# Attention with its strided units first, and expert 0 in three groups of 384 tokens

## The chip, the cores and the metric

One core of one Trainium2 chip runs the whole program. The metric is the device time of one execution in microseconds (us). The engines are called as in the profile: PE is the matrix engine (PEld its weight loads), DVE the vector engine, ACT the scalar engine, POOL the general one, and SP the engine whose queue issues most of the transfers (DMAs).

## The reference

Three layers follow each other. Attention has 2 batches, 8 heads, 576 positions of width 64; heads 0 to 3 see the last 32 positions ("local"), heads 4 to 7 see the earlier positions of the same class modulo 32 ("strided"). The 1152 rows of width 512 that come out of it go through a dense mixture of 8 experts, weighted by a matrix P that 8 rounds of row and column scaling make. Its result goes through a second mixture that picks two experts for each token.

```python
scores = scale * np.matmul(q, k.transpose(0, 1, 3, 2))            # per head, masked local or strided
attn = softmax(np.where(masks, scores, -1e9))
x = np.matmul(attn, v)                                            # -> [1152, 512]
logits = x @ w_gate
P = np.exp(logits - logits.max())
for _ in range(8):
    P /= P.sum(1, keepdims=True) + 1e-09
    P /= P.sum(0, keepdims=True) + 1e-09
    P *= N / E
for e in range(E):
    out += P[:, e:e + 1] * (np.maximum(x @ w1[e], 0.0) @ w2[e])   # 8 experts, all tokens
...                                                               # then the layer with the two best experts
```

## The kernel before

**Precision.** Each product of the experts is three matmuls: `split` (L99) makes a high and a low part of an operand (ACT writes the high part at L101 or L104, DVE the low part at L102 or L106), and `mm3` (L162) multiplies high with high, low with high and high with low.

**Attention** is cut into units. A `local_unit` (L262) is one batch, one pair of heads and three blocks of 64 queries; a `strided_unit` (L282) is one batch, both strided pairs of heads and four (the last time three) blocks of 54. A unit goes through: scores on PE into a bank of PSUM (`scores`, L223), the maximum on DVE (L241), an exponential on ACT for each block (L247), the scaling on DVE (L251), a transpose on PE (L271 or L290), a copy by ACT or DVE (L258, L260), the product with the values on PE (L277, L298), and `split` into `xh` and `xl`, whose four chunks are the two local and the two strided pairs. A batch has six local units (three of pair 0, then three of pair 1) and then three strided ones; `attention(0)` stands ahead of `attention(1)` (L316). Ahead of the first scores PE does 16 filler matmuls (`hum`, L219).

**Loads.** `load_pair` (L186) issues q, k and the values of a pair as transfers of their own on SP's queue, which goes in order: a transfer whose place is not free yet holds up those behind it. The first pair of batch 0 comes in two cuts. The local queries, and the strided ones of batch 1, lie in the part of `acc` (from its fifth tile of 128 tokens on) that is not used yet.

**Expert 0** of the dense layer runs beside attention. Its inner width 1024 is cut into four quarters `q`: `fetch_u` loads 1 MB of weights, `conv_u1` and `conv_u2` split them, `pair1` (L621) makes hidden values for a group of tokens, `pair2` (L630) adds their product to `acc`, tile by tile. First come all four quarters for the `early` tokens 0 to 511 (tiles 0 to 3), behind `attention(1)` in the program; then the gate (`gate_logits`, `sinkhorn`: eight rounds that make P); then the four quarters again for the `late` tokens in two groups of 320 (tiles 4 to 8). The conversions of quarter 0 stand on ACT behind the ninth `split` (`firsts[8]`), a split of the second strided unit of batch 0, and those of quarter 1 and later behind the twelfth.

**Sums.** Experts 1 to 6 use products of quarter blocks, for which `sums` (L667) makes four sums of the blocks of x in two steps `c`: eight additions on DVE into `r`, then four `split`s of it. Both steps' splits stand on ACT behind the second late quarter (`marks[1]`), and their work on DVE behind the first `split` of the hidden values (`lows[0]`).

**Order.** Up to the last expert of the dense layer, the order of each engine's instructions is made when the program is built, by priority (program order, with the gate and `sinkhorn` raised) and modelled times; what is emitted in the end runs in order on each engine. `issue_after` adds an edge on one engine only: an instruction that stands in its block waits for one that is named, if both are on the same engine.

Of the kernel before, what the change touches and what calls it, by code (L numbers as in the profile page):

```python
# [59 lines left out]


@with_exitstack
def tile_kernel(ctx: ExitStack, tc: tile.TileContext, qL, kL, vL, qS, kS, vS, wg, u12, w1, w2, wgn, noise, v1, v2, cst, masks, dummy, out):
    nc = tc.nc
    cpool = ctx.enter_context(tc.tile_pool(name="cpool", bufs=1))
    dram = ctx.enter_context(tc.tile_pool(name="dram", bufs=1, space=bass.MemoryType.DRAM))
# [111 lines left out]
    fold2 = cpool.tile([128, 2 * E], F32, name="fold2")  # L178
    fold = apool.tile([64, E], F32, name="fold", bufs=1)
    flip = [0, 0]  # L180
    where = [0, "ad", None]
    spread = [apool.tile([128, 4, 2, 64], F32, name=f"spread{i}", bufs=1) for i in range(2)]
    for x in spread:
        nc.gpsimd.memset(x, 0.0)

    def load_pair(b, hp):  # L186
        local = hp < 2
        nq, nk, nb, q, k, v = (NQ, LK, NJ, qL, kL, vL) if local else (GK, GK, NG, qS, kS, vS)
        hp %= 2
        flip[1] = (flip[1] + 1) % 4  # L190
        qs = acc[:, 4:].rearrange("p t d -> p (t d)")[:, flip[1] * 640:flip[1] * 640 + nb * nq]
        w = k.shape[-1]
        if b == 0 and not local:
            qs = pre.tile([128, NG * GK], F32, name=f"qs{hp}")
            ks = pre.tile([128, S + STRIDE], F32, name=f"ks{hp}")
        else:
            ks = apool.tile([128, S + STRIDE], F32, tag="ks", name="ks")
        if local or hp == 0:
            where[2] = (pre if b == 0 and not local else apool).tile([128, NG, 128], F32, tag="vs", name="vs")
        vs, n = where[2], v.shape[-2]  # L200
        if b == 0 and hp == 0 and local:
            cut = 3 * nq
            nc.sync.dma_start(ks[:, :224], k[b, hp, :, :224])
            nc.sync.dma_start(qs[:, :cut], q[b, hp, :, :cut])
            nc.sync.dma_start(ks[:, 224:w], k[b, hp, :, 224:])
            nc.sync.dma_start(qs[:, cut:], q[b, hp, :, cut:])
        else:
            nc.sync.dma_start(ks[:, :w], k[b, hp])
            nc.sync.dma_start(qs, q[b, hp])

        def values():
            if local:
                nc.sync.dma_start(vs[:, :n], v[b, hp])
            elif hp == 1:
                nc.sync.dma_start(vs[:, :n], v[b])

        return (qs, ks, vs), values

    def hum(o, n):  # L219
        for _ in range(n):  # L220
# [38 lines left out]
        else:  # L259
            nc.vector.tensor_copy(o, i)  # L260

    def local_unit(b, hp, j0, nb, got):  # L262
        qs, ks, vs = got
        first = maskb[:, M_ML:M_MS].rearrange("p (b k) -> p b k", b=3)
        mask = first if j0 == 0 else first[:, 1:2].to_broadcast([128, nb, LK])
        scv = scores(NQ, LK, mask, j0, nb, qs, ks, NQ)
        s = apool.tile([128, 1, 3, LK], F32, tag="s", name="s", bufs=3)
        weights_of([scv], s)
        tr = ps("b", "tr")
        for i in range(nb):  # L270
            nc.tensor.transpose(tr[:LK, i * 128:(i + 1) * 128], s[:, 0, i], ident)  # L271
        at = apool.tile([128, 4 * 2 * GK], F32, tag="at", name="at", bufs=3)
        take(at, tr, LK, NQ, nb)
        ot = ps("c", "ot")
        for i in range(nb):
# [6 lines left out]
    def strided_unit(b, j0, nb, pairs):  # L282
        mask = maskb[:, None, M_MS:].to_broadcast([128, nb, GK])
        scv = [scores(GK, GK, mask, j0, nb, qs, ks, GK) for qs, ks, _ in pairs]
        vs = pairs[0][2]
# [19 lines left out]
    def load_first():  # L305
        pairs, queue = [], []
        for hp in range(4):
            got, values = load_pair(0, hp)
            pairs.append(got)
            if queue:  # L310
                queue.pop(0)()
            queue.append(values)
        queue.pop()()
        return pairs

    def attention(b):  # L316
        pairs = load_first() if b == 0 else []

        def get(hp):
            while hp >= len(pairs):  # L320
                got, values = load_pair(b, len(pairs))
                values()
                pairs.append(got)
            return pairs[hp]

        for hp in range(2):
            for j0, nb in LOCAL:
                local_unit(b, hp, j0, nb, get(hp))
        get(3)
        for j0, nb in STRIDED:  # L330
            strided_unit(b, j0, nb, pairs[2:])

    mask_sb = apool.tile([128, NMASK // 2], F32, name="mask_sb", bufs=1)
    nc.scalar.dma_start(mask_sb, masks)
# [15 lines left out]
    nc.gpsimd.tensor_tensor(fold2, ident[:, :2 * E], ident[:, 32:32 + 2 * E], op=ALU.add)  # L350
    for j in (64, 96):
        nc.gpsimd.tensor_tensor(fold2, fold2, ident[:, j:j + 2 * E], op=ALU.add)
    where[1] = "a"
    attention(1)
    split(wg2[:, :, :E], wg2[:, :, 32:32 + E], wg_sb)

# [258 lines left out]
        return xg  # L615

    whole = ((0, 384), (384, 384), (768, 384))
    early = ((0, 512),)
    late = ((512, 320), (832, 320))

    def pair1(w, groups):  # L621
        wh, wl = w
# [23 lines left out]

    for q in range(NP):
        raw = fetch_u(0, q)
        with tc.issue_after(firsts[min(q, 1) * 3 + 8].ins):
            a, b = conv_u1(raw[0]), conv_u2(raw[1])  # L650
        pair1(a, early)
        for t in range(4):
            pair2(b, t, None, q == 0)
    tags[:] = ["a", "c"]
    with tc.high_priority(1500):
# [11 lines left out]
    def sums():  # L667
        with tc.tile_pool(name="tpool", bufs=1, side="right", reuse_waits="tile") as tpool:
            for c in range(2):
                r = tpool.tile([128, 4, HALF], F32, tag="r", name="r")  # L670
                for i in range(4):
                    nc.vector.tensor_tensor(r[:, i], quarter[0][i][:, c].bitcast(F32), quarter[1][i][:, c].bitcast(F32), op=ALU.add)
                for o, x, y, op in ((3, 2, 3, ALU.add), (2, 0, 2, ALU.subtract), (0, 3, 0, ALU.subtract), (1, 1, 0, ALU.subtract)):
                    nc.vector.tensor_tensor(r[:, o], r[:, x], r[:, y], op=op)
                for k, i in enumerate((3, 0, 2, 1)):
                    split(sh[:, k, c], sl[:, k, c], r[:, i])

    marks = []
    for q in range(NP):
        q = NP - 1 - q  # L680
        if q < NP - 1:
            raw = fetch_u(0, q)
            a, b = conv_u1(raw[0]), conv_u2(raw[1])
        pair1(a, late)
        for t in range(4, NT):
            pair2(b, t, None, q == NP - 1)
        marks.append(seen[0].ins)
    with tc.issue_after(marks[1]), tc.issue_after(lows[0].ins):
        sums()
    with tc.issue_after(seen[0].ins):  # L690
        nc.scalar.dma_start(wgn_sb, wgn)
        nc.scalar.dma_start(noise_sb, noise)
# [438 lines left out]
                down(ws[2:], [tt], [OVER], 0)  # L1131


_HOST = ["qL", "kL", "vL", "qS", "kS", "vS", "wg", "u12", "w1", "w2", "wgn", "noise", "v1", "v2", "cst", "masks", "dummy"]


def layout(x):
# [10 lines left out]
    def keys(a):  # L1148
        return a.transpose(0, 1, 3, 2).reshape(B, 2, 2 * D, a.shape[2])
# [25 lines left out]
    for j in range(3):  # L1175
# [15 lines left out]
    d = dict(qL=keys(q[:, :4]), kL=keys(kL), vL=values(vL, LK, NQ),  # L1191
             qS=keys(qS), kS=keys(kS), vS=values(vS, GK, GK).reshape(B, 128, NG, 2 * D), wg=rows(x["moe_w_gate"]),
             u12=np.stack([x["moe_w1"].reshape(E, NC, 128, NP, 256).transpose(0, 3, 2, 1, 4).reshape(E, NP, 128, 2, 512),
                           x["moe_w2"].reshape(E, NP, 2, 128, DM).transpose(0, 1, 3, 2, 4)], 3).reshape(E, NP, 128, 4, 512),
             w1=w1t(x["moe_w1"])[E - 1:], w2=w2t(x["moe_w2"])[E - 1:],
# [19 lines left out]
```

## Time and profile before

| | us |
|---|---|
| median of 3 runs (lowest to highest) | 1104.33 (1103.67 to 1104.60) |
| the profiled execution, its own time | 1105.53 |
| its span in the trace | 1103.7 |
| PE busy in the span | 1085.4 |
| DVE busy | 661.6 |
| ACT busy | 396.5 |

The trace covers the span; 1.8 us of the profiled execution's time lie around it. "Busy" is the union of an engine's instructions; of a matmul the end is modelled. The granted clock is 1.00 at 2.4 GHz and falls to 0.5 at 1.2 GHz, so that a mean of 0.9 over a stretch says that a fifth of it was at the lower level. Stages of interest: attention until about 83 us, the early part of expert 0 from 33.8 to 103.7 us, the late part until about 163 us, and experts 1 to 6 after it.

### The profile page before, as it was taken

The numbers are of one execution on the slowest core, as the hardware profiler recorded it, in microseconds if no ns is written. First come the engines' busy times: TensorE is split into PE (matmuls) and PEld (weight loads), VectorE is DVE, ScalarE is ACT, GpSimd is POOL, SyncE is SP. The second block draws the span as 40 slices with busy tenths as digits, with TensorE's granted clock in tenths as the row PEclk, the third lists the DMA queues.
The fourth block names the chain that finished last, engine by engine and source line by source line (L and its number), as shares of the span: only waits on it lengthen the run. The fifth ranks groups of instructions, "written<-read, shape, count | busy, mean of one in ns | idle before, by whom it ended". The sixth has DMA issues, their size and how long they took to land.

```text
span 1103.7 us, 17178 instructions
## 1 busy us (share of the span) xinstructions
PE 1085.4 (98%) x6840; PEld 954.5 (86%) x6840; DVE 661.6 (60%) x1359; ACT 396.5 (36%) x893; POOL 158.8 (14%) x182
## 2 busy tenths in 40 slices
PE   9999999999999999999999999999999999999996
PEld 6778988999899999899999999988888888888885
DVE  6865896666666666666666666554266465445440
ACT  6641334332322333322332332222133254444541
POOL 1000112111111111121111120000041432232211
PEclk9999999999999999999999999999999999999998
DMA  9321162111111121111121111122103674666531
GB/s 349 133 77 39 39 198 67 39 71 44 40 39 39 39 78 39 39 39 39 39 77 39 39 39 39 39 77 77 39 21 125 181 256 106 205 204 205 185 99 24
DMA packets 31589, 98.18 MB, mean 89 GB/s; under 512 B 6482, under 2 KB 15186, under 8 KB 22928
## 3 DMA queue, kind: packets, MB, share of 16 engines
q1 hardware_dynamic: 16192, 78.94, 19.7%
q0 software_dynamic: 5408, 11.26, 4.9%
q10 hardware_dynamic: 9904, 6.83, 2.0%
q8 instruction: 55, 0.90, 0.3%
q14 instruction: 30, 0.25, 0.1%
HBM read 85.51 MB, written 11.60 MB: 88 GB/s over the span
## 4 chain that ended last, share of the span: by engine, by line
PE 90%; DVE 3%; DMA 2%; ACT 2%; issue 1%; POOL 1%; POOLq 0%; SPq 0%; ACTq 0%
PE y L164 42%; PE h L164 17%; PE a L715 14%; PE b L715 7%; PE d L715 3%; PE y L892 2%; PE xgt L800 1%; PE sc L232 1%; ACT spread L247 1%; DMA raw<-in_v 1%; DMA xg<-x2d,tt 1%; DVE wl L106 1%; PE sc L221 0%; POOL table L548 0%; PE lgT L367 0%
## 5 line engine op out<-in xcount | busy, mean ns | idle before, releaser
L641 DVE SCALAR_TENSOR_TENSOR acc<-y,P,acc 128x512 f32<-128x512 f32 x207 | 152.8, 748 | 142.8 <-PE y L164 142.7
L164 PE MATMUL y<-u2h,gh 128*128 128x512 f32 x504 | 199.0, 395 | 0.6 <-DVE acc L641 0.3
L164 PE MATMUL y<-u2l,gh 128*128 128x512 f32 x504 | 197.8, 392 | 0.0
L164 PE MATMUL y<-u2h,gl 128*128 128x512 f32 x504 | 190.6, 393 | 0.8 <-DVE gl L102 0.8
L154 POOL TENSOR_TENSOR ut<-raw 128x256 f32<-128x256 f32 x48 | 36.5, 782 | 554.0 <-DVE u1l L106 446.0
L164 PEld LDWEIGHTS y<-u2h,gl 128*128 128x128 f32 x504 | 94.8, 189 | 20.8 <-DVE gl L102 1.6
L164 PE MATMUL h<-xh,wh 128*128 128x384 f32 (+8 forms) x352 | 110.2, 313 | 0.2 <-DVE hl L102 0.2
L164 PE MATMUL h<-xl,wh 128*128 128x384 f32 (+8 forms) x352 | 110.2, 313 | 0.0
L164 PE MATMUL h<-xh,wl 128*128 128x384 f32 (+8 forms) x352 | 109.8, 312 | 0.0
L164 PEld LDWEIGHTS y<-u2h,gh 128*128 128x128 f32 x504 | 95.1, 189 | 16.2 <-issue 0.7
L164 PEld LDWEIGHTS y<-u2l,gh 128*128 128x128 f32 x504 | 95.0, 188 | 14.1
L101 ACT ACTIVATE hh<-h 128x256 fp32r<-128x256 f32 (+2 forms) x88 | 35.6, 415 | 95.5 <-PE h L164 95.5
L164 PEld LDWEIGHTS h<-xh,wh 128*128 128x128 f32 x352 | 66.4, 189 | 1.1 <-DVE hl L102 0.5
L164 PEld LDWEIGHTS h<-xl,wh 128*128 128x128 f32 x352 | 66.4, 189 | 0.9 <-issue 0.4
L104 ACT ACTIVATE u2h<-raw 128x1024 fp32r<-128x1024 f32 x31 | 33.0, 1064 | 94.5 <-PE y L164 90.8
L164 PEld LDWEIGHTS h<-xh,wl 128*128 128x128 f32 x352 | 66.4, 189 | 0.0
L102 DVE SCALAR_TENSOR_TENSOR hl<-h,hh 128x256 fp32r<-128x256 f32 (+2 forms) x88 | 40.3, 465 | 41.2 <-ACT hh L101 41.2
L106 DVE TENSOR_TENSOR wl<-raw,wh 128x1024 fp32r<-128x1024 f32 x42 | 49.5, 1221 | 22.8 <-ACT wh L104 22.8
L715 PE MATMUL b<-sh,u1h 128*128 128x288 f32 x192 | 57.5, 299 | 0.0
L715 PE MATMUL b<-sl,u1h 128*128 128x288 f32 x192 | 57.5, 299 | 0.0
L715 PE MATMUL b<-sh,u1l 128*128 128x288 f32 x192 | 57.4, 299 | 0.0
L715 PE MATMUL a<-sh,u1l 128*128 128x288 f32 x192 | 57.0, 297 | 0.0
(257 smaller groups left out, 2453.9 us busy)
## 6 DMA issues: line engine op xcount, KB each, us to landing
raw<-in_u SPq DMA_DIRECT2D x31, 1024.0 KB, 4.8
raw<-in_v SPq DMA_DIRECT2D x20, 1024.0 KB, 8.9
acc<-in_v SPq DMA_DIRECT2D x12, 1024.0 KB, 6.8
raw<-in_w SPq DMA_DIRECT2D x4, 1024.0 KB, 4.9
out<-zero ACTq DMA_DIRECT2D x1, 3072.0 KB, 18.2
vs<-in_vL SPq DMA_DIRECT2D x4, 576.0 KB, 7.1
x2d<-acc ACTq DMA_DIRECT2D x9, 256.0 KB, 2.0
vs<-in_vS SPq DMA_DIRECT2D x2, 704.0 KB, 6.5
```

Source lines behind the costliest of these rows:

```text
L101: seen[0] = nc.scalar.activation(hi, src, AF.Relu)
L102: lows.append(nc.vector.scalar_tensor_tensor(lo, src, 0.0, hi.bitcast(F32), op0=ALU.max, op1=ALU.subtract))
L104: seen[0] = nc.scalar.activation(hi, src, AF.Copy)
L106: nc.vector.tensor_tensor(lo, src, hi.bitcast(F32), op=ALU.subtract)
L154: nc.gpsimd.tensor_tensor(t[:, o], x, y, op=ALU.subtract)
L164: nc.tensor.matmul(o, a, b, start=start, stop=stop)
L232: nc.tensor.matmul(sc[h * 64:h * 64 + w, i * nk:(i + 1) * nk], qs[r, j * w:(j + 1) * w], ks[r, j * step:j * step + nk], start=False, stop= ...
L247: nc.scalar.activation(s[:, x, i], v[:, i], AF.Exp, scale=0.125, bias=nmx[:, k:k + 1], accum_out=sm[:, k:k + 1])
L641: nc.vector.scalar_tensor_tensor(acc[:, t], p, P[:, t, scale:scale + 1], acc[:, t], op0=ALU.mult, op1=ALU.add)
L715: nc.tensor.matmul(p, l[:, b, c], m, start=first and i == 0, stop=i == 5, skip_group_check=not first)
L800: nc.tensor.transpose(p[:, o:o + 128], xg[:, c * 128:(c + 1) * 128], ident)
L892: nc.tensor.matmul(p[j * w:j * w + k, :d], hr[:, f, :k], raws[f // 4][:, f % 4, j * d:(j + 1) * d], start=f == 0, stop=f == 7)
```

## The change

- `attention(b)` does the three strided units first, then the local units by block group: both pairs of heads for blocks 0 to 2, then for blocks 3 to 5, then for 6 to 8.
- q and k of a pair come in one transfer into one tile (`xS`, `xL`, laid out on the host): the strided ones in tiles of their own, in batch 0 cut so that the columns of the first unit come first; the local ones in the free part of `acc`. There are three tiles for values.
- The scores take PSUM banks of one tag only (`where[1] = "a"`) from the second local group of batch 0 on (before: from batch 1 on).
- Expert 0's tokens are grouped as 384 early (tiles 0 to 2) and two times 384 late (tiles 3 to 8).
- The conversions of quarter 0 stand behind the fifth and the seventh `split`, later quarters' behind the eleventh.
- `sums` is ordered in two steps: the splits of step c on ACT behind `marks[c]`; the edge to `lows[0]` on DVE is gone.

```diff
-    def load_pair(b, hp):
...
+    def load(x, src, cut=0):
+        if cut:
+            nc.sync.dma_start(x[:, :, :cut], src[:, :, :cut])
+            return partial(nc.sync.dma_start, x[:, :, cut:], src[:, :, cut:])
+        nc.sync.dma_start(x, src)
+
+    def load_strided(b):
+        xs, rest = [], []
+        for hp in range(2):
+            if b == 0:
+                x = pre.tile([128, 2, NG * GK], F32, name=f"x{hp}")
+            else:
+                x = apool.tile([128, 2, NG * GK], F32, tag="x", name="x")
+            rest.append(load(x, xS[b, hp], (1 - b) * STRIDED[0][1] * GK))
+            xs.append(x)
+        for f in rest:
+            if f:
+                f()
+        vs = (pre if b == 0 else apool).tile([128, NG, 128], F32, tag="vs", name="vs", bufs=1 if b == 0 else 3)
+        return xs, vs, partial(nc.sync.dma_start, vs, vS[b])
+
+    def load_local(b):
+        xs, vs = [], []
+        for hp in range(2):
+            x = acc[:, 4:].rearrange("p t d -> p (t d)")[:, hp * 1280:hp * 1280 + 2 * S + STRIDE]
+            load(x, xL[b, hp])
+            xs.append((x[:, :S], x[:, S:]))
+        for hp in range(2):
+            v = apool.tile([128, NG, 128], F32, tag="vs", name="vs", bufs=3)
+            load(v[:, :NJ], vL[b, hp])
+            vs.append(v)
+        return xs, vs
...
     def attention(b):
-        pairs = load_first() if b == 0 else []
...
-        for hp in range(2):
-            for j0, nb in LOCAL:
-                local_unit(b, hp, j0, nb, get(hp))
-        get(3)
+        xs, vs, values = load_strided(b)
+        values()
+        lx, lv = load_local(b)
         for j0, nb in STRIDED:
-            strided_unit(b, j0, nb, pairs[2:])
+            strided_unit(b, j0, nb, xs, vs)
+        for j0, nb in LOCAL:
+            if j0:
+                where[1] = "a"
+            for hp in range(2):
+                local_unit(b, hp, j0, nb, *lx[hp], lv[hp])
...
-    where[1] = "a"
     attention(1)
...
     whole = ((0, 384), (384, 384), (768, 384))
-    early = ((0, 512),)
-    late = ((512, 320), (832, 320))
+    early = whole[:1]
+    late = whole[1:]
...
-        with tc.issue_after(firsts[min(q, 1) * 3 + 8].ins):
-            a, b = conv_u1(raw[0]), conv_u2(raw[1])
+        with tc.issue_after(firsts[10 if q else 4].ins):
+            a = conv_u1(raw[0])
+        with tc.issue_after(firsts[10 if q else 6].ins):
+            b = conv_u2(raw[1])
         pair1(a, early)
-        for t in range(4):
+        for t in range(3):
             pair2(b, t, None, q == 0)
...
             for c in range(2):
-                r = tpool.tile([128, 4, HALF], F32, tag="r", name="r")
...
+                with tc.issue_after(marks[c]):
+                    r = tpool.tile([128, 4, HALF], F32, tag="r", name="r")
...
         pair1(a, late)
-        for t in range(4, NT):
+        for t in range(3, NT):
             pair2(b, t, None, q == NP - 1)
         marks.append(seen[0].ins)
-    with tc.issue_after(marks[1]), tc.issue_after(lows[0].ins):
-        sums()
+    sums()
```

## Rows read from the trace of the kernel before

**Rows 1.** Busy us of PE, PEld, DVE, ACT, POOL by stretch; then clock, DMA.
```profile
6.20:20.00 13.80, 13.30 (x235) 10.04 (x234) 10.11 (x42) 10.47 (x59) 0.00 (x0) 1.00 1.04 412
20.00:33.80 13.80, 12.19 (x206) 9.03 (x203) 12.04 (x41) 12.41 (x61) 1.04 (x5) 0.92 0.66 246
33.80:61.00 27.20, 27.20 (x245) 20.93 (x244) 21.30 (x52) 14.53 (x55) 0.00 (x0) 0.98 0.44 155
61.00:73.00 12.00, 10.76 (x120) 7.96 (x118) 8.08 (x19) 7.61 (x36) 0.00 (x0) 0.86 0.01 1
73.00:103.70 30.70, 30.70 (x170) 23.71 (x168) 18.32 (x33) 6.26 (x10) 0.00 (x0) 1.00 0.20 70
103.70:128.00 24.30, 24.30 (x145) 22.57 (x145) 15.71 (x49) 5.74 (x12) 0.05 (x1) 1.00 0.13 44
128.00:142.00 14.00, 13.98 (x78) 12.33 (x77) 13.54 (x24) 5.94 (x11) 3.78 (x4) 1.00 0.03 5
142.00:158.00 16.00, 15.42 (x88) 13.60 (x87) 15.76 (x35) 6.89 (x12) 4.44 (x4) 1.00 0.61 195
158.00:180.00 22.00, 20.10 (x113) 17.71 (x112) 16.77 (x47) 7.58 (x16) 3.90 (x4) 0.92 0.61 188
```

**Rows 2.** Waits of PE until 240 us: total us, times, longest.
```profile
PE cs L395 <- DVE c L393: 1.5, 1, 1.5
PE sc L227 <- ACT spread L247: 1.1, 2, 0.6
```

**Rows 3.** Chain of waits, pieces in order of time: start us, us, what.
```profile
86.15 2.76 PE y L164 x12
...
91.22 5.60 PE h L164 x24
...
108.38 1.76 PE h L164 x12
```

**Rows 4.** The tile ot: all 24 low parts, first and last start.
```profile
L106 DVE TENSOR_TENSOR xl<-ot,xh x24: 305/389/564, 14.8 to 83.4; 128x192 fp32r<-128x192 f32 x12, 128x216 fp32r<-128x216 f32 x8, 128x144 fp32r<-128x144 f32 x4
```

**Rows 5.** Timeline of PE and of ACT: first matmul of expert 0, first exponential.
```profile
33.83 0.78 PE L164 MATMUL h<-xh,u1h 128*128 128x512 f32 x1
...
8.18 0.34 ACT L247 ACTIVATE s<-sc,nmx 128x96 f32<-128x96 f32 x1 [6.16 <-DVE nmx L242]
```

**Rows 6.** Group of the local exponentials, 6 to 34 us: busy us, mean ns.
```profile
L247 ACT ACTIVATE s<-sc,nmx 128x96 f32<-128x96 f32 x27 | 8.8, 353 | 6.4 <-DVE nmx L242 6.2 <-DVE sm L248 0.3
```

**Rows 7.** Groups of DVE, 33.8 to 103.7 us: busy us, mean ns, idle before.
```profile
L645 DVE TENSOR_TENSOR acc<-y,acc 128x512 f32<-128x512 f32 x12 | 8.2, 686 | 5.1 <-PE y L164 5.1
L106 DVE TENSOR_TENSOR u2l<-raw,u2h 128x1024 fp32r<-128x1024 f32 x5 | 6.1, 1220 | 0.4 <-ACT u2h L104 0.4
L106 DVE TENSOR_TENSOR u1l<-raw,u1h 128x512 fp32r<-128x512 f32 x9 | 6.0, 684 | 2.7 <-ACT u1h L104 2.7
L102 DVE SCALAR_TENSOR_TENSOR gl<-h,gh 128x512 fp32r<-128x512 f32 x8 | 5.5, 686 | 6.5 <-ACT gh L101 6.5
```

**Rows 8.** The tile r of the sums: times of one, first and last start.
```profile
L672 DVE TENSOR_TENSOR r<-xh,xl x8: 741/745/753, 42.0 to 138.7; 128x576 f32<-128x576 f32 x8
...
L104 ACT ACTIVATE sh<-r x8: 667/672/691, 129.2 to 147.3; 128x576 fp32r<-128x576 f32 x8
L106 DVE TENSOR_TENSOR sl<-r,sh x8: 741/746/1292, 131.4 to 151.8; 128x576 fp32r<-128x576 f32 x8
```

**Rows 9.** The matmul of each round of sinkhorn, two instructions a round.
```profile
L395 PE MATMUL cs<-c,onesr x16: 170/256/278, 110.2 to 171.1; 128*128 128x8 f32 x16
```

**Rows 10.** SP's queue in order of time, and its DMA issues by size.
```profile
1.65 0.42 SPq L205 DMA_DIRECT2D ks<-in_kL  x1
...
12.12 1.07 SPq L133 DMA_DIRECT2D raw<-in_u  x2
13.66 0.33 SPq L208 DMA_DIRECT2D ks<-in_kL  x1
...
ks<-in_kL SPq DMA_DIRECT2D x1, 192.0 KB, 3.8
```

More of the change, by code (lines that the diff above doesn't have):

```diff
@@ L62, in tile_kernel @@
 @with_exitstack
-def tile_kernel(ctx: ExitStack, tc: tile.TileContext, qL, kL, vL, qS, kS, vS, wg, u12, w1, w2, wgn, noise, v1, v2, cst, masks, dummy, out):
+def tile_kernel(ctx: ExitStack, tc: tile.TileContext, xL, vL, xS, vS, wg, u12, w1, w2, wgn, noise, v1, v2, cst, masks, dummy, out):
     nc = tc.nc
@@ L180, in tile_kernel @@
     flip = [0, 0]
-    where = [0, "ad", None]
+    where = [0, "ad"]
     spread = [apool.tile([128, 4, 2, 64], F32, name=f"spread{i}", bufs=1) for i in range(2)]
@@ L184, in tile_kernel @@
         nc.gpsimd.memset(x, 0.0)
-    def load_pair(b, hp):
[L187 to L217, printed above, removed]
@@ L260, in take, with local_unit @@
             nc.vector.tensor_copy(o, i)
-    def local_unit(b, hp, j0, nb, got):
-        qs, ks, vs = got
+    def local_unit(b, hp, j0, nb, qs, ks, vs):
         first = maskb[:, M_ML:M_MS].rearrange("p (b k) -> p b k", b=3)
@@ L280, in local_unit, with strided_unit @@
         split(xh[:, hp, o], xl[:, hp, o], ot[:, :nb * NQ])
-    def strided_unit(b, j0, nb, pairs):
+    def strided_unit(b, j0, nb, xs, vs):
         mask = maskb[:, None, M_MS:].to_broadcast([128, nb, GK])
-        scv = [scores(GK, GK, mask, j0, nb, qs, ks, GK) for qs, ks, _ in pairs]
-        vs = pairs[0][2]
+        scv = [scores(GK, GK, mask, j0, nb, x[:, 0], x[:, 1], GK) for x in xs]
         wide = spread[where[0] // 2 % 2]
@@ L303, in strided_unit @@
             split(view[0][:, r0:r1], view[1][:, r0:r1], ot[:, :(r1 - r0) * NI].rearrange("p (r i) -> p r i", i=NI))
[L305 to L314, printed above, removed]
-    def attention(b):
-        pairs = load_first() if b == 0 else []
[L319 to L324, printed above, removed]
-        for hp in range(2):
-            for j0, nb in LOCAL:
-                local_unit(b, hp, j0, nb, get(hp))
-        get(3)
-        for j0, nb in STRIDED:
-            strided_unit(b, j0, nb, pairs[2:])
+    def attention(b):
+        xs, vs, values = load_strided(b)
+        values()
+        lx, lv = load_local(b)
+        for j0, nb in STRIDED:
+            strided_unit(b, j0, nb, xs, vs)
[4 more added lines that the diff above has]
+                local_unit(b, hp, j0, nb, *lx[hp], lv[hp])
     mask_sb = apool.tile([128, NMASK // 2], F32, name="mask_sb", bufs=1)
@@ L669, in sums @@
             for c in range(2):
-                r = tpool.tile([128, 4, HALF], F32, tag="r", name="r")
[L671 to L676, printed above, removed]
+                with tc.issue_after(marks[c]):
+                    r = tpool.tile([128, 4, HALF], F32, tag="r", name="r")
+                    for i in range(4):
+                        nc.vector.tensor_tensor(r[:, i], quarter[0][i][:, c].bitcast(F32), quarter[1][i][:, c].bitcast(F32), op=ALU.add)
+                    for o, x, y, op in ((3, 2, 3, ALU.add), (2, 0, 2, ALU.subtract), (0, 3, 0, ALU.subtract), (1, 1, 0, ALU.subtract)):
+                        nc.vector.tensor_tensor(r[:, o], r[:, x], r[:, y], op=op)
+                    for k, i in enumerate((3, 0, 2, 1)):
+                        split(sh[:, k, c], sl[:, k, c], r[:, i])
     marks = []
@@ L1131, in tile_kernel @@
                 down(ws[2:], [tt], [OVER], 0)
-_HOST = ["qL", "kL", "vL", "qS", "kS", "vS", "wg", "u12", "w1", "w2", "wgn", "noise", "v1", "v2", "cst", "masks", "dummy"]
+_HOST = ["xL", "vL", "xS", "vS", "wg", "u12", "w1", "w2", "wgn", "noise", "v1", "v2", "cst", "masks", "dummy"]
 def layout(x):
@@ L1190, in layout @@
     dummy[:, 0] = np.arange(E * ROWS) % ROWS % PAD
-    d = dict(qL=keys(q[:, :4]), kL=keys(kL), vL=values(vL, LK, NQ),
-             qS=keys(qS), kS=keys(kS), vS=values(vS, GK, GK).reshape(B, 128, NG, 2 * D), wg=rows(x["moe_w_gate"]),
+    d = dict(xL=np.concatenate([keys(q[:, :4]), keys(kL)], 3), vL=values(vL, LK, NQ),
+             xS=np.stack([keys(qS), keys(kS)], 3), vS=values(vS, GK, GK).reshape(B, 128, NG, 2 * D), wg=rows(x["moe_w_gate"]),
              u12=np.stack([x["moe_w1"].reshape(E, NC, 128, NP, 256).transpose(0, 3, 2, 1, 4).reshape(E, NP, 128, 2, 512),
```

## The prediction

> **What bounds the kernel now.** I read the stretches first, then what ends PE's waits, then single tiles. Over the span PE is busy 1085.4 of 1103.7 us, and the change touches only the first 180 us or so, so the question is how much of PE's time there is idle or at the lower clock. [rows 1] gives it. From 6.2 to 33.8 us PE is idle 0.50 + 1.61 = 2.1 us, and the granted clock 0.92 in the second stretch stands for 0.16 x 13.8 = 2.2 us at the lower level, so 1.1 us of work lost: 3.2 us together. From 33.8 to 61 us nothing is idle (0.5 us lost to the clock). From 61 to 73 us it is 1.24 idle and (1 - 0.86) x 12 = 1.7 to the clock, 2.9 together. From 73 to 142 us, nothing to speak of. From 142 to 180 us it is 0.58 + 1.90 idle and 0.08 x 22 = 1.8 to the clock: 4.2 together. The lower level, 1.2 in place of 2.4 GHz, comes each time in a stretch in which PE also pauses. All that a better order of the same work can win is 3.2 + 0.5 + 2.9 + 4.2 = 10.8 us.
>
> Who holds PE up differs by stage. Until 33.8 us, when expert 0's first matmul starts [rows 5], ACT and DVE carry the attention (ACT 12.41, DVE 12.04 of 13.8 us [rows 1]). At 61 to 73 us PE waits for the banks of strided scores, which ACT's exponentials free [rows 2]. From 128 to 158 us DVE is full (13.54 of 14 and 15.76 of 16 us), after only 15.71 of 24.3 us in the stretch ahead of it [rows 1]; the longest wait is for sinkhorn's column sum on DVE, 1.5 us [rows 2].
>
> **PE's own work: no change.** A matmul of 512 columns takes 5.60/24 = 0.2333 us and one of 320 takes 1.76/12 = 0.1467 us [rows 3]; on the line through both, 384 columns take 0.1754 us. A hidden value is 12 matmuls a group, 8 times: before 96 x (0.2333 + 2 x 0.1467) = 50.6 us, after 96 x 3 x 0.1754 = 50.5. The tiles of `pair2` stay nine a quarter at 2.76/2 = 1.38 us each [rows 3]. What moves is the balance: early work was 96 x 0.2333 + 16 x 1.38 = 44.5 us and becomes 96 x 0.1754 + 12 x 1.38 = 33.4 us; late work grows by the same 11.1.
>
> **The start: about 0.5 us won.** Expert 0 now needs seven of batch 0's nine units, not all. ACT is busy 22.9 us between its first exponential at 8.2 us and 33.8 us [rows 1, 5], idle 2.7. Of this 9 of the 27 local exponentials (8.8 x 9/27 = 2.9 us [rows 6]) are of batch 1, and about 2.4 us quarter 0's conversions (taken as DVE's halves of them, 2 x 0.68 + 1.22 [rows 7], a little less). The two units that may come later are 6 exponentials (2.0 us) and about 1 us of copies. So the first matmul can come at 8.2 + (22.9 - 2.9 - 2.4 - 3.0) + 2.4 + 2.7 = 27.9 us, 5.9 us earlier. This is not 5.9 us won: PE was busy 25.5 of those 27.6 us with attention, some of it batch 1's, and what isn't done by 28 us is done later. Only the 3.2 us of waste can go. The strided units come first with 8 exponentials ahead of the first transpose, which gives PE less to do early; so I take 0.5, between -2 (the first 14 us, with 0.5 us idle now, get as thin as the next 14) and +3.2.
>
> **The loads: nothing.** The first unit now needs two transfers of 128 x 432 x 4 B = 216 KB in place of some 208 KB. The third transfer of before (400 KB in all by then) was issued at 1.65 us and landed 3.8 us later, at 5.45 us [rows 10]; 432 KB land by about 5.6, and the fillers keep PE until 6.2 us. The cover is 0.6 us thin; without it each 0.1 us costs 0.1. Later transfers follow at 412 GB/s [rows 1]: the rest of q and k and the strided values by 10 us, all 4.3 MB of batch 0 by about 15, ahead of the local units, which ACT reaches after 22 strided exponentials. Batch 1's strided tiles no longer share a place with local ones, so those two waits of SP go.
>
> **The middle: 1.5 us won.** After 28 us PE has 33.4 us of early work and about 20 us of attention left: PE's busy time from 6.2 to 103.7 us less the losses, the early work and the gate's matmuls leaves some 40 us for both batches, and 18 to 20 of it are done by 28 us. So it lasts until about 82 us. DVE's share of that: one batch and two units, about 17.5 + 3, and of the experts 12 additions (0.6 each to the next), 8 low parts (about 0.47) and three quarters' conversions [rows 7], 18: together 38.5 of 54 us, 71%, as 47.7 of 69.9 us, 68%, now [rows 1]. The burst of strided exponentials that held PE up at 61 us still comes, three times, but at about 30 to 45 us, while two quarters of hidden values lie ready as filler. I take half of 2.9, between -3 (DVE is late with hidden values) and +2.9.
>
> **The sums: 3.8 us won.** r is there from 42 us on, but its first split on ACT starts only at 129.2 us, behind the second late quarter, and the second step follows until 152 us [rows 8]: 8 low parts, 4 second-step additions and 4 combinations, 16 x 0.7 = 11 us of DVE in a stretch where it is full, with sinkhorn's rounds between them (16 matmuls from 110.2 to 171.1 us, 7.6 us a round [rows 9]). After the change the first step's splits come behind the first late quarter, one quarter or 8.4 + 8.3 = 16.7 us of PE time earlier than behind the second, and the second step's additions with them. The gate comes earlier too, since batch 1 ends earlier, so sinkhorn should be done before the sums of expert 1 are wanted, and the wait of 1.5 us with the slow clock behind it goes. Late work is 11.1 us longer on PE, so DVE has more time in all. I take 3.8 of 4.2, between 0 and 4.2. The dropped edge to `lows[0]` costs at most two additions of 0.7 us early on; DVE has room.
>
> **Sum.** 0.5 + 1.5 + 3.8 = 5.8 us. Against the profiled execution's own 1105.5 (1103.7 of span and 1.8 around it) that is 1099.7; the median of the runs is 1.2 us below that execution, so 1098.5. The bounds of the parts give +5 and -10.3; the forecast's own range is 1095 to 1102.
>
> **A rule that says more.** PEld is busy 10.04 of 13.8 and 9.03 of 13.8 us in the attention, 73% and 65%, but 22.57 of 24.3, 93%, where only experts run [rows 1]. If the small matmuls leave such room, PE's 97% before 20 us is no bound, and the 5.9 us of the earlier start count in full: 5.9 + 1.5 + 3.8 = 11.2, 1093. The Trainium skill, "Perfetto Trace Analysis", section "Identifying the Most-Contended Engine", says that the busy share of matmuls is a poor measure of headroom and that the busy share of weight loads should be read instead.
>
> **Rivals.**
> - *More, 1093* (12%): as just worked out. Against it: the waits of PE before 33.8 us are only 2 us.
> - *Given back, 1104* (18%): DVE's load is only moved, and what the sums leave at 150 us comes back at 28 to 60 us, where all of batch 1 (20.5 us with the two units) and two quarters of expert work (9 us) want DVE in 32 us, 92%. Then 3.8 + 0.5 is met by 3 to 4 of new waits for low parts. For it: PE's wait for DVE's low parts is the pattern of 142 to 158 us. Against it: from 33.8 to 61 us DVE was at 78% without an idle PE.
> - *Slower, 1107.7* (15%): batch 1's local q and k go into places that batch 0's last local scores read, and these now come last, at about 25 us. If the planner puts those transfers ahead of quarter 0's or 1's weights on SP, the queue stands until then, 2.4 MB take 5.9 us, the weights 2.5 us a quarter and 2 to land, the conversions 2.4: the first matmul comes at 38 us, not 28. PE has some 4 of the 10 us filled by batch 1's strided units and loses about 1.2 to the clock: 6 + 1.2 - 3.8 = 3.4 us slower, 1107.7. It decides from the point where the weights are issued behind about 20 us. Against it: before, the weights (12.12 us) went ahead of transfers that stand earlier in the program (13.66) [rows 10]. The same sign has the case that early work ends before batch 1 does: its last low part came at 83.4 us [rows 4], 49.6 us after expert 0's start, and with the same lag comes at 77.5, 4.5 us ahead of 82.
>
> **Numbers.** Forecast 55%. Faster by over 0.2% (2.2 us, about what a measurement of this kernel can tell from none) is 0.53 of the forecast's 0.55, the 0.12 and a little of "given back": 0.67. Same: most of "given back", 0.17. Slower: 0.16. A range that leaves out some 10% at each end is 1092 to 1107.5.
>
> **What would show it.** Right: expert 0's first matmul at 26 to 30 us; the first `sh` split near 95 us in place of 129.2; sinkhorn's last matmul before 150 us; PE idle under 0.5 us in the last late quarter and at expert 1's start. Wrong: raw weights landing after 25 us; PE waiting for `gl` or for `spread` at 30 to 60 us; a pause of PE between the early and the late part; a mean clock below 0.9 in any of these.

## The result and the profile after

| | before | after |
|---|---|---|
| median of 5 runs (lowest to highest), us | 1104.33 (1103.67 to 1105.72) | 1114.23 (1109.55 to 1115.20) |
| ratio, with its 95% interval | | 1.0081 (1.0061 to 1.0100) |
| the profiled execution, own time / span, us | 1105.53 / 1103.7 | 1115.20 / 1113.4 |
| mean granted clock over the span | 0.992 | 0.984 |

The change makes the kernel 0.8% slower, some 9.9 us by the medians; 1098.5 was forecast. Most of it is lost before 200 us. The same stretches as in [rows 1], and one more:

```profile
6.20:20.00 13.80, 11.99 (x185) 8.56 (x183) 7.62 (x29) 9.03 (x57) 0.00 (x0) 0.88 1.03 419
20.00:33.80 13.80, 11.29 (x160) 8.26 (x160) 10.03 (x33) 8.89 (x37) 0.00 (x0) 0.76 0.54 205
33.80:61.00 27.20, 26.77 (x273) 21.14 (x270) 18.48 (x49) 17.58 (x77) 2.26 (x5) 0.74 0.36 128
61.00:73.00 12.00, 12.00 (x140) 9.50 (x139) 10.43 (x31) 7.30 (x27) 0.00 (x0) 1.00 0.24 89
73.00:103.70 30.70, 30.28 (x197) 24.45 (x196) 21.24 (x45) 8.65 (x24) 0.00 (x0) 1.00 0.19 69
...
128.00:142.00 14.00, 14.00 (x72) 12.65 (x72) 12.64 (x25) 5.50 (x10) 3.33 (x4) 1.00 0.69 216
142.00:158.00 16.00, 16.00 (x83) 14.63 (x82) 12.63 (x31) 4.56 (x8) 2.94 (x4) 1.00 0.67 201
158.00:180.00 22.00, 20.28 (x115) 18.07 (x114) 16.94 (x48) 5.95 (x11) 2.87 (x4) 1.00 0.26 96
180.00:200.00 20.00, 20.00 (x110) 17.96 (x109) 11.22 (x22) 10.16 (x21) 2.87 (x4) 0.91 0.01 1
```

Read PE's busy time (the first number behind the length) and the clock (the third from the end) against [rows 1]. From 6.2 to 61 us PE is idle 1.81 + 2.51 + 0.43 = 4.8 us, where it was 2.1 before, and the clock takes (0.12 + 0.24) x 13.8 + 0.26 x 27.2 = 12.0 us, where it took 1.6. That is 13.1 us more lost. From 61 to 73 us nothing is lost any more: 2.9 us won, more than forecast. At 128 to 158 us DVE is no longer full and PE never idle. But the wait behind it has only moved: 1.72 us idle at 158 to 180, again for sinkhorn's column sum (`cs`, last line of the waits below), and 0.09 x 20 = 1.8 us of clock behind that, 3.5 in place of 4.2. Together with 0.4 us idle at 73 to 104 us the sum is 13.1 - 2.9 - 0.7 + 0.4 = 9.9 us. Counted from one event to the same event it is less: the 100th matmul of expert 1's products starts at 197.2 us instead of 188.8, which is 8.4 us, and the last 1.3 of the span's 9.7 us arise later. What lies between the 9.9 and the 8.4 us is not explained.

The clock's largest piece is one unbroken stretch at the lower of its two levels:

```profile
30.70:47.80 17.10, 16.67 (x145) 12.82 (x146) 11.58 (x29) 9.90 (x38) 2.26 (x5) 0.50 0.47 166
```

PE is busy 16.67 of its 17.10 us, so in a view of busy time this stretch looks full; it takes the granted clock to see that the work runs at half speed. PE's timeline shows the pauses for banks of scores that came before it, and what ended it (start, duration, instruction, and in brackets the pause ahead of it):

```profile
10.98 0.23 PE L227 MATMUL sc<-mask_sb 128*128 128x162 bf16 x1 [0.59 <-ACT spread L247]
...
12.13 0.23 PE L227 MATMUL sc<-mask_sb 128*128 128x162 bf16 x1 [0.48 <-ACT spread L247]
...
13.27 0.28 PE L227 MATMUL sc<-mask_sb 128*128 128x288 bf16 x1 [0.48 <-ACT spread L247]
...
21.44 0.28 PE L227 MATMUL sc<-mask_sb 128*128 128x288 bf16 x1 [0.57 <-ACT s L247]
...
28.97 0.25 PE L227 MATMUL sc<-mask_sb 128*128 128x216 bf16 x1 [0.56 <-ACT s L247]
...
30.43 0.25 PE L227 MATMUL sc<-mask_sb 128*128 128x216 bf16 x1 [0.67 <-ACT s L247]
...
36.64 1.01 PE L164 MATMUL h<-xh,u1h 128*128 128x384 f32 x2 [0.43 <-ACT xh L104]
37.58 1.55 PE L276 MATMUL ot<-at,vs 96*64 96x64 f32 x24
...
46.71 0.52 PE L164 MATMUL h<-xh,u1l 128*128 128x384 f32 x1
47.03 0.52 PE L164 MATMUL h<-xh,u1h 128*128 128x384 f32 x1
...
48.43 0.34 PE L164 MATMUL h<-xl,u1h 128*128 128x384 f32 x1
48.61 0.34 PE L164 MATMUL h<-xh,u1l 128*128 128x384 f32 x1
```

Two pauses of 0.56 and 0.67 us for banks of scores come right ahead of it. Through it PE runs the attention's matmuls of 54 to 96 columns, its transposes and masks, and a few of expert 0's between them. Most of expert 0's are recorded with 0.52 us each here, and with 0.34 us at full clock. The clock is back at 47.8 us, after expert 0's matmuls of 384 columns have run in one piece since 46.23 us. The first of them, which was to start at 27.9 us, starts at 36.64 (before: 33.83 [rows 5]).

PE's longest waits until 50 us (total, times, longest) are for what ACT's exponentials free, strided (`spread`) and local (`s`); the last line is the wait for sinkhorn between 150 and 200 us:

```profile
PE sc L227 <- ACT s L247: 1.8, 3, 0.7
PE sc L227 <- ACT spread L247: 1.6, 3, 0.6
...
PE cs L376 <- DVE c L374: 1.7, 1, 1.7
```

The sums did move. The splits of r start at 115.9 us in place of 129.2, and the last low part starts at 139.2 in place of 151.8 us [rows 8]; yet sinkhorn's last matmul, at 171.1 us before [rows 9], is at 179.3 now:

```profile
L104 ACT ACTIVATE sh<-r x8: 669/672/675, 115.9 to 135.9; 128x576 fp32r<-128x576 f32 x8
L106 DVE TENSOR_TENSOR sl<-r,sh x8: 742/746/747, 118.1 to 139.2; 128x576 fp32r<-128x576 f32 x8
...
L376 PE MATMUL cs<-c,onesr x16: 170/256/277, 108.9 to 179.3; 128*128 128x8 f32 x16
```

### The profile page after: what moved, and what is told of

Same layout as the page of the kernel before. It is cut to its first block, busy times and chain, and to the rows that moved or that the text cites. A ratio compares the mean times of both kernels' runs of the same rounds, so it can differ in the third digit from the quotient of the medians.

```text
span 1113.4 us, 17155 instructions
## 1 busy us (share of the span) xinstructions
PE 1092.7 (98%) x6840; PEld 963.5 (87%) x6840; DVE 662.9 (60%) x1359; ACT 396.6 (36%) x893; POOL 156.6 (14%) x182
## 4 chain that ended last, share of the span: by engine, by line
PE 91%; DVE 3%; DMA 2%; ACT 1%; issue 1%; POOL 1%; POOLq 0%; SPq 0%; ACTq 0%
PE y L164 42%; PE h L164 17%; PE a L698 14%; PE b L698 7%; PE d L698 3%; PE y L875 2%; PE sc L232 1%; PE xgt L783 1%; DMA xg<-x2d,tt 1%; DMA raw<-in_v 1%; PE ot L276 1%; DVE wl L106 1%; PE sc L221 1%; POOL table L529 1%; ACT spread L247 0%
## 5 line engine op out<-in xcount | busy, mean ns | idle before, releaser
L698 PE MATMUL a<-sh,u1h 128*128 128x288 f32 x192 | 57.1, 297 | 0.0
```

The costliest lines, as they stand in the source:

```text
L698: nc.tensor.matmul(p, l[:, b, c], m, start=first and i == 0, stop=i == 5, skip_group_check=not first)
```

## The experiments

Ratios are to the kernel before on the same chip, with 95% intervals. The kernel before itself had medians of 1105.24, 1104.68 and 1106.97 us beside the three groups of runs, so medians of different groups are not compared directly, only the ratios.

### Which part of the change costs it

**The sums in two steps alone**, on the kernel before:

```diff
             for c in range(2):
+                with tc.issue_after(marks[c]):
...
-    with tc.issue_after(marks[1]), tc.issue_after(lows[0].ins):
-        sums()
+    sums()
```

> The kernel before with one part of the change alone: the sums in two steps (each step's splits behind its own late quarter, no edge on DVE). If the forecast of the sums holds, DVE's full stretch after 128 us thins out and the 4.2 us that PE loses at 142 to 180 us shrink to about 0.4: 1100.5, ratio 0.9965. If sinkhorn's last rounds stay just ahead of expert 1's sums whatever the sums do, the wait for its column sum and the slow clock behind it stay, and the time is 1103 to 1104.5 (ratio 0.999 to 1.000). If the two steps themselves cost time, it is over 1106.

Measured: 1103.92 us, 0.9994 (0.9984 to 1.0003). No difference that the interval allows to call one.

**The groups of 384 alone**, on the kernel before:

```diff
-    early = ((0, 512),)
-    late = ((512, 320), (832, 320))
+    early = whole[:1]
+    late = whole[1:]
```

> The kernel before with one part alone: expert 0 in groups of 384 (early tiles 0 to 2). Attention as before, local units first. Theory that attention's new order is what costs: this kernel is within 2 us of before, 1102 to 1106, first matmul of expert 0 near 33 us, lower-clock time in the first 60 us near 3.4 us as before. Rival that the shorter early work (33.4 in place of 44.5 us) leaves PE without filler: PE pauses at 60 to 95 us, at least one more stretch at the lower clock, 1108 to 1114.

Measured: 1106.16 us, 1.0012 (1.0003 to 1.0022): at most 0.2% slower.

**The change without the groups** (the edit above, backwards, on the changed kernel):

> The changed kernel with the old token groups (512, then 320 and 320). If attention's new order and its banks are the cause, the slow stretch before 50 us stays and the time is 1109 to 1116, like the changed kernel. If the short early group is the cause, the time comes back to 1100 to 1105.

Measured: 1113.29 us, 1.0081 (1.0065 to 1.0098), the same as the whole change. So the 0.8% lie in what is left of it: the attention's order, loads and banks, and the places of the conversions. The loss is made up otherwise, though. In the three stretches from 6.2 to 61 us

```profile
6.20:20.00 13.80, 10.70 (x195) 7.62 (x193) 8.34 (x32) 10.32 (x65) 0.00 (x0) 1.00 1.03 420
20.00:33.80 13.80, 10.56 (x167) 7.67 (x166) 10.89 (x32) 9.28 (x34) 0.00 (x0) 0.88 0.57 207
33.80:61.00 27.20, 25.94 (x291) 20.01 (x292) 19.96 (x53) 17.02 (x74) 0.80 (x5) 0.87 0.37 128
```

PE is idle 7.6 us, where the whole change has 4.8, and the clock takes 5.2 us, where it took 12.0.

**The change with both tags of banks through batch 0**, as before:

```diff
-            if j0:
-                where[1] = "a"
...
+    where[1] = "a"
     attention(1)
```

> The changed kernel, but the scores of all of batch 0 use the banks of both tags, as before, and one tag only from batch 1 on. Theory that the two banks from the second local group on serialize scores and exponentials (PE waited three times for the local and three times for the strided exponentials, then ran 17 us at the lower clock): first matmul of expert 0 at 28 to 31 us in place of 36.6, lower-clock time before 60 us falls from 24 to 3 to 10 us, time 1101 to 1106. Rival that strided units first starve PE by themselves (eight exponentials ahead of the first transpose): pauses at 10 to 15 us stay, first matmul of expert 0 at 34 us or later, time 1109 to 1115.

Measured: 1117.91 us, 1.0128 (1.0094 to 1.0162), slower than either expectation. That batch 0's later local units take banks of one tag is not the cause: with the second tag there (batch 1 has one tag in both kernels) the kernel is slower still, with PE idle 1.57 + 3.79 + 3.12 us in the three stretches from 6.2 to 61 us and a clock of 0.75 in the last of them.

### The order of attention, batch by batch

**Local units first in both batches**, still by block group, still with the merged transfers. The first strided transfer is not cut, quarter 0's conversions stand behind the ninth split and the later ones' behind the twelfth, and the scores take one tag of banks from batch 1 on, all as this order needs it or as before:

```diff
-            strided_unit(b, j0, nb, xs, vs)
...
+        lx, lv = load_local(b)
+        xs, vs, values = load_strided(b)
+        values()
+        local(lx, lv)
+        strided(xs, vs)
```

> The changed kernel with its merged transfers, its groups of 384 tokens and its sums in two steps, but in both batches the local units (still by block group, both pairs behind each other) and their loads come ahead of the strided ones. Theory (the strided-first order costs: TensorE pauses on the strided units' exponentials, the attention's small matmuls then run at the lower clock, and expert 0's fill starts late): about 1103 to 1106 us, ratio 0.999 to 1.002, first matmul of expert 0 at 33 to 35 us and no 17 us stretch at the lower clock. Rival (merged transfers or the order by block group cost it): 1111 to 1114 us, ratio 1.006 to 1.009.

Measured: 1108.83 us, 1.0032 (1.0022 to 1.0042), between the two expectations.

**The same in batch 0 alone** (batch 1 keeps its strided units first):

> As the kernel with local units first, but for batch 0 alone; batch 1 keeps its strided units first. Theory (what is lost is lost in batch 0, before 50 us): the same 1103 to 1106 us as with both batches local first. Rival (batch 1's order costs, through the fill between 50 and 104 us): 1109 to 1114 us, and the better time only where both batches are turned.

Measured: 1104.64 us, 0.9993 (0.9982 to 1.0003). Batch 0's order carries the loss: with local units first there, and with everything else of the change kept but the edits named above, all of the 0.8% is gone. The merged transfers and the order by block group are cleared. The uncut transfer and the later conversions were not tested apart from the order; the kernel with fillers (below) has both as the change has them, and loses nothing.

The two runs also test the forecast's first step. With both batches turned, expert 0's first matmul starts at the time that the forecast hoped for (33 to 35 us were expected of this run), and 6.4 us earlier than with batch 0 alone turned (28.04 against 34.45 us):

```profile
28.04 0.44 PE L164 MATMUL h<-xh,u1h 128*128 128x384 f32 x1
```

It is still the slower of the two by 4 us. Until 158 us both lose the same, 4.7 us of idle time and 6.8 us at the lower clock, so the early start of expert 0 has won nothing there. They differ at 158 to 180 us, first with both turned, then with batch 0 alone:

```profile
158.00:180.00 22.00, 18.02 (x99) 16.41 (x98) 16.35 (x51) 5.17 (x11) 2.88 (x4) 0.84 0.14 49
```
```profile
158.00:180.00 22.00, 20.29 (x118) 18.43 (x118) 16.07 (x45) 6.33 (x15) 2.87 (x4) 0.92 0.14 49
```

### Clock or order

My theory until then was that the late start of expert 0 cost the time, and the clock a part. **Fillers** tell these apart: about 30 matmuls of 512 columns on ones, without a use, behind the scores of batch 0's units in the changed kernel. They add work, and can win only through the clock and the pauses, or through another order of PE's instructions (tested below).

```diff
+    def warm(tag, n):
+        with tc.issue_after(last[0].ins):
+            hum(ps(tag, "hm"), n)
...
+        if b == 0:
+            warm("d", 3)        # local_unit
...
+        if b == 0:
+            warm("c", 4)        # strided_unit
```

> The changed kernel with about 30 more filler matmuls in batch 0: four behind each strided unit's scores, three behind each local unit's, some 7 us of TensorE work by the fillers' own pitch. They add no result. Rival (the clock alone costs it: the pauses of 10 to 30 us lower the clock, and the work at the lower clock is the loss): the 17 us at the lower clock go, and the time falls to 1105 to 1109 us although work was added. Theory (order and late fill cost it, the clock is only a part): 1112 to 1119 us, the lower clock shorter by some of its 17 us and the first matmul of expert 0 no earlier than 36 us.

Measured: 1104.94 us, 0.9999 (0.9989 to 1.0009). My theory fell, and the time is the rival's: with 30 x 0.216 = 6.5 us of useless work added, the kernel is some 9 us faster, though expert 0's first matmul still comes at 34.46 us. The lower clock is gone from the whole stretch, and PE has no pause left from 33.8 to 61 us (the first three stretches of [rows 1], in the kernel with fillers):

```profile
6.20:20.00 13.80, 13.02 (x196) 8.39 (x194) 8.77 (x33) 10.41 (x62) 0.00 (x0) 1.00 1.03 416
20.00:33.80 13.80, 13.03 (x197) 9.01 (x196) 11.27 (x33) 9.99 (x45) 0.00 (x0) 1.00 0.60 217
33.80:61.00 27.20, 27.20 (x348) 22.20 (x348) 22.96 (x64) 21.11 (x88) 0.80 (x5) 1.00 0.47 166
```

Two more kernels ask whether it is their work that counts, or only that the planner now orders PE's instructions otherwise (it does: attention's instructions stand in a somewhat different order with fillers).

**The same 30 fillers, 32 columns wide**:

```diff
-            hum(ps(tag, "hm"), n)
+            p = ps(tag, "hm")
+            for _ in range(n):
+                nc.tensor.matmul(p[:, :32], onesb, onesb[:, :32], start=True, stop=True)
```

> The same 30 added matmuls at the same places as in the run with fillers, but 32 columns wide instead of 512, so that they add next to no work and hardly fill a pause. Theory (the lower clock is what the change lost, and the wide fillers kept it up by keeping TensorE at work): the lower clock is back for 10 us or more before 50 us, and the time is 1108 to 1116 us. Rival (the fillers helped by shifting the order in which TensorE's instructions were put, not by the clock): as fast as with wide fillers or, with their 7 us of work gone, faster: 1097 to 1105 us.

Measured: 1113.42 us, 1.0053 (1.0036 to 1.0071). Without their work the fillers leave most of the loss, and the lower clock is back for 13.6 us:

```profile
20.00:33.80 13.80, 12.71 (x169) 9.92 (x168) 9.25 (x28) 7.67 (x30) 0.00 (x0) 0.63 0.56 210
33.80:61.00 27.20, 25.17 (x293) 19.58 (x288) 20.40 (x54) 18.31 (x78) 0.80 (x5) 0.94 0.37 128
```

This control isn't perfect: its order is neither of the others', and it has a wait of its own of 1.8 us for a bank.

**Twelve wide fillers, behind the local units alone** (two each):

> Fillers of 512 columns behind the local units of batch 0 alone, two each: 12 instead of 30, some 2.8 us of work instead of 7. Theory (it is the pauses between 20 and 30 us, where the local units run, that bring the 17 us at the lower clock): the long stretch stays away with these too, and 1099 to 1104 us. Rival (the pauses of the strided units at 10 to 20 us are what counts, or more fillers are needed): the lower clock lasts 7 us or more between 20 and 50 us, 1105 to 1115 us.

Measured: 1112.34 us, 1.0045 (1.0031 to 1.0060). A miss for my guess of the place: the clock fell at 12.0 us already, for 6.8 us, so the pauses of the strided units count as well, or twelve are too few.

**The 30 fillers in the kernel before**:

> The kernel before with the same 30 fillers behind the scores of batch 0's units (three for each local unit, four for each strided one). Theory (they win what the changed kernel lost to the clock, and the kernel before lost little there: 6.8 us at the lower clock ahead of 160 us, 3.4 us in time): 1104 to 1109 us, their 7 us of work less what lies in pauses and less 3 us of clock. Rival (fillers win some 9 us in any kernel of this kind): 1094 to 1099 us.

Measured: 1109.88 us, 1.0020 (1.0008 to 1.0031), just above the expected range. Where little is lost to the clock, fillers cost 0.2%. So their 0.8% in the changed kernel is no gift that any kernel would get; it is what the change had lost to pauses and clock.

**Batch 0 local first, and four fillers behind each of its strided units**:

> Batch 0 with its local units first, all else as changed, and four fillers behind each strided unit of batch 0 (12, some 2.8 us of work), where that kernel paused at 27.7 and 29.7 us and then had 6.8 us at the lower clock. Theory (clock): that stretch goes, and 1100 to 1104 us, the fillers' work about paid for by 3.4 us of clock and the filled pauses. Rival: 1105 to 1108 us, the fillers' work on top.

Measured: 1103.84 us, 0.9970 (0.9960 to 0.9981). It is the one version that computes everything and beats both kernels, by 0.3% the kernel before. No stretch at the lower clock is left ahead of 167 us:

```profile
6.20:20.00 13.80, 13.80 (x250) 10.53 (x249) 11.05 (x46) 11.56 (x66) 0.81 (x4) 1.00 1.02 420
20.00:33.80 13.80, 12.40 (x212) 9.06 (x209) 10.29 (x30) 11.43 (x57) 2.69 (x5) 1.00 0.71 282
33.80:61.00 27.20, 26.07 (x301) 20.55 (x300) 23.83 (x63) 19.71 (x79) 0.13 (x2) 1.00 0.33 117
```

One account holds for all of these. P is the start of the 100th matmul of expert 1's products. Ahead of it all kernels run the same 1438 recorded matmuls (1432 are recorded with both tags of banks) and their fillers, save for the width of expert 0's groups before and with the old groups. From P the table takes PE's idle time since 6.2 us, half of the time at the lower clock (half of the work is lost in it) and the fillers (0.216 us for a wide one, some 0.03 for a narrow one):

| kernel | P | idle | at the lower clock | fillers | rest |
|---|---|---|---|---|---|
| before | 188.8 | 5.8 | 10.2 | 0 | 177.9 |
| before, sums alone | 187.9 | 6.9 | 6.8 | 0 | 177.6 |
| before, groups alone | 189.5 | 7.0 | 6.8 | 0 | 179.1 |
| before, fillers | 191.6 | 3.5 | 3.4 | 6.5 | 179.9 |
| after | 197.2 | 6.9 | 27.3 | 0 | 176.6 |
| after, old groups | 195.0 | 11.2 | 13.7 | 0 | 177.0 |
| after, both tags of banks | 200.5 | 11.0 | 23.9 | 0 | 177.5 |
| local first, both batches | 191.8 | 8.7 | 13.6 | 0 | 176.3 |
| local first, batch 0 | 187.9 | 6.4 | 10.2 | 0 | 176.4 |
| the same, fillers | 185.1 | 4.7 | 3.4 | 2.6 | 176.1 |
| after, fillers | 188.7 | 3.7 | 3.4 | 6.5 | 176.8 |
| after, narrow fillers | 193.1 | 8.7 | 13.6 | 0.9 | 176.7 |
| after, 12 fillers | 193.4 | 7.6 | 13.6 | 2.6 | 176.4 |

The rest is the same within 1.4 us for all nine kernels with the new attention, while P differs by 15. So idle time and clock together account for what sets them apart. Of the change's 8.4 us at P the clock is (27.3 - 10.2) / 2 = 8.6, the idle time 1.1, and the rest, -1.3, goes the other way. Where those 1.3 us come from, and why fillers in the kernel before add 2 us more than their own time, I have not settled.

The division between clock and pauses is that of one execution, and it does not carry over. With the old groups, as slow by its ratio, the clock is 1.7 and the idle time 5.4 of the 6.2 us at P. And the fastest execution of the changed kernel has a mean clock of 0.994, above the 0.992 of before's profiled one, yet takes 1109.55 us where that took 1105.53: the lower clock can't account for that difference. It left no trace, so where those 4 us went is open. What is shown is that pauses and lower clock make up the loss together, and that filling the pauses with work removes it.

### Where the gain of the sums went

**The sums in two steps on the kernel before, and five rounds of sinkhorn instead of eight** (three rounds of P's scaling are left out):

```diff
-        for _ in range(8):
+        for _ in range(5):
```

> The kernel before with the sums in two steps alone, and five instead of eight rounds of the iteration that scales P (three rounds are left out). Theory (the relief of VectorE was given back because the last of those rounds are what TensorE waits for ahead of expert 1's sums: 4.5 us idle and the 6.8 us at the lower clock behind it): 1096 to 1100 us, ratio 0.993 to 0.996, no wait on c and no lower clock near 167 us. Rival (the relief was never on the path): 1102.5 to 1104.5 us, ratio 0.998 to 1.000.

Measured: 1096.44 us, 0.9919 (0.9899 to 0.9940). With eight rounds and the early sums PE stands still for 5.0 us at 158 to 180 us and loses 0.16 x 22 = 3.5 us to the clock; with five, nothing. DVE isn't full there (14.68 of 22 us). First PE's longest wait and this stretch with eight rounds, then the stretch with five:

```profile
PE cs L395 <- DVE c L393: 4.5, 2, 2.3
...
158.00:180.00 22.00, 16.98 (x99) 15.53 (x98) 14.68 (x46) 5.81 (x13) 2.69 (x4) 0.84 0.14 48
```
```profile
158.00:180.00 22.00, 22.00 (x138) 20.38 (x137) 15.33 (x28) 11.65 (x24) 5.04 (x8) 1.00 0.14 48
```

These 8.5 us answer to what the five rounds gain over the eight, 0.9994 - 0.9919 = 0.75%, or 8.3 us. So the sums do not end the stage; sinkhorn's last rounds do. Until 158 us that kernel loses 1.9 us to pauses and nothing to the clock, where before lost 3.9 and 3.4, most of it ahead of 128 us; so PE comes sooner to the same rounds and waits longer for them: 4.5 us where it was 1.5 [rows 2]. The kernel with the groups alone, whose sums stand as before, waits nearly as long:

```profile
PE cs L395 <- DVE c L393: 3.8, 2, 2.3
```

Whether the rounds can be made to end sooner by the order on DVE alone was not tried.

## Why the prediction was wrong, point by point

- **What bounds the kernel: right in kind.** The forecast counted pauses and clock by stage, and the account above finds the differences between the kernels there, within 1.4 us. It also wrote that the lower level "comes each time in a stretch in which PE also pauses", and then priced it as an appendage of the pause, of 1 to 2 us.
- **"The start: about 0.5 us won", between -2 and +3.2: the step that failed.** It was 13.1 us lost from 6.2 to 61 us. It failed twice. First the start itself: ACT was taken to be as busy as before, idle 2.7 us until expert 0 begins. It was busy only 9.03 + 8.89 = 17.9 of 27.6 us, and DVE 7.62 + 10.03 = 17.7 us. That fits a chain of scores, maximum, exponential and transpose in which the engines wait for one another, since a strided unit comes first with little beside it; no run tests this by itself. The first matmul came at 36.64, not 27.9 us. Then the bound: -2 was made from the next stretch of the trace, "the first 14 us get as thin as the next 14", which has pauses of 1.61 us and a clock of 0.92. A thin stretch can leave the clock down over the full stretch behind it, here for 17.1 us. The rows of before show a trace of this, a clock of 0.98 at 33.8 to 61 us with PE never idle, and the bound had no term for it.
- **"A rule that says more": did not come true.** PEld was busy 73% and 65% in the first two stretches [rows 1], and by the rule that was room. After the change it is 62% and 60%, and PE got less done. The Trainium skill, "Perfetto Trace Analysis", section "Identifying the Most-Contended Engine", calls the busy share of matmuls a poor measure and names that of weight loads, beside the FLOPs done, in its place. PE's busy share did mislead here, 16.67 of 17.10 us at half the clock; but the share of weight loads didn't show what could be won either.
- **The loads: right that they don't decide.** Quarter 0's raw weights were issued at 9.19 us, ahead of the transfers that wait for a place, and with the merged transfers kept, the kernel with batch 0 local first is as fast as before. The cover did end: the first exponential comes at 9.67 us, 8.18 before [rows 5]. But the fillers ahead of the first scores ran longer in this execution too, so the runs don't give the transfers' share.
- **The middle: right, and more.** 2.9 us won, 1.5 were forecast: PE is busy 12.00 of 12.00 us at 61 to 73 us. But the kernels with the sums or the groups alone have the same 12.00 there, so the attention's order is not needed for it. (In its sums, 384 columns lie at 0.1756, not 0.1754 us, and the experts' share of DVE adds up to 18.7, not 18; neither matters.)
- **The sums: 3.8 us forecast, 0.7 came.** The splits moved from 129.2 to 115.9 us, not to 95, and DVE got its room; "sinkhorn should be done before the sums of expert 1 are wanted" is the step that failed, as the runs with eight and five rounds show. Rows for it stood ready: 7.6 us a round, and the wait for its column sum [rows 2, 9].
- **The rivals.** "Slower, 1107.7" had the sign and a first matmul at 38 us, close to 36.64, but neither the cause nor the price, so the nearness is luck: SP's queue did stand until 26.19 us for batch 1's local tiles, but quarter 0's weights were issued ahead of them, at 9.19 us, and its "about 1.2 to the clock" was 12.0. "Given back" has the time of the sums alone by luck: what was given back there went to sinkhorn's rounds, not to DVE's load at 28 to 60 us. The list of signs had "a mean clock below 0.9": the clock was 0.88, 0.76 and 0.74 in the first three stretches, but no rival was built on that sign.

## What to carry over

Where small matmuls that depend on other engines are put in a row, price the granted clock as a term of its own beside the pauses: it may stay down over the full stretch that follows them, and in the busy time it cannot be seen. Useless wide matmuls in the pauses are a cheap test of the two together, with narrow ones at the same places as the control; the same fillers cost 0.2% in the kernel before, which lost little to the clock there. When a stage's load is taken off an engine, look for the chain that ends the stage next, here eight rounds of a small iteration, before counting the load as won.

## What the runs showed of the hardware

- PE stayed at the lower level for 17.1 us in which it was busy 97% of the time by the records, with the attention's small matmuls and a few wide ones between them. No pause between 6.2 us and that stretch was longer than 0.7 us. The Trainium skill, "TensorE: Matmul & The Clock Gate", section "A second HAM failure mode: psum-queue depth-cycling", tells of short pauses between groups of matmuls that bring the clock down again; the trace agrees, with pauses of 0.48 to 0.67 us for banks of scores. But pauses of that size do not always bring it down: the kernel with the groups alone has four of 0.35 to 0.66 us ahead of 31 us, and a clock of 1.00 until 61 us.
- The share of the lower level differs between executions of one program. After's five runs have mean clocks of 0.994, 0.988, 0.989, 0.985 and 0.984 and took 1109.55, 1112.10, 1114.23, 1114.30 and 1115.20 us, a spread of 5.7 us, where before's five lie within 2.1. The profiled execution, on which the account above rests, is the slowest of them.
- A matmul's recorded duration, whose end is modelled, grows less than the step from one to the next: at the lower level one of 384 columns is recorded with 0.52 us instead of 0.34, while the step went from 0.18 to 0.32 us (48.43 to 48.61 and 46.71 to 47.03 us in the timeline above). So a stretch's loss is read from the steps or from the clock, not from durations.
